# A batch's first two output tiles share their steps, and the first transfers come in another order

## The chip, the cores and the metric

The kernel runs on one core of one Trainium2 chip. The time is the device time of one execution in microseconds (us). Six engines' rows occur here: PE (TensorE's matmuls), PEld (its weight loads), DVE (VectorE), ACT (ScalarE), POOL (GpSimd) and SP (SyncE, which issues most of the transfers; SPq is its queue). Each engine works off its own instructions in the order in which the program lists them, and semaphores hold an instruction back until what it needs is there.

## The reference

```python
# q, k, v: 8 batches, 12 heads, 448 tokens, 64 dims, float32
scores = q @ k.transpose(0, 1, 3, 2) / sqrt(64) - log(448)
x = (sigmoid(scores) @ v)                  # per head
x = x.transpose(0, 2, 1, 3).reshape(3584, 768)
h = x @ w_in                               # 768 x 2048
g = where(h > 0, h, exp(min(h, 0)) - 1)
out = g @ w_out                            # 2048 x 768
```

## The kernel before

**Tiling.** A batch's 448 tokens are three chunks of 128 (`NC` = 3) and a rest of 64; the rests of two batches share one tile. Heads go in pairs, six a batch (`hp` = 0 to 5, `n` counts the pairs over all batches). For a pair, PE multiplies q by k (tile `psc`, L663), ACT takes the sigmoid into `sg` (L687), ACT and DVE turn that into `at` (L698, L699), and PE multiplies `at` by the values (`pav`, L712). After a batch's six pairs its hidden layer follows: PE makes `h` (L1006), and ACT and DVE turn it into `g` in 16 blocks `f` (L1032, L1038); the last quarter, blocks 12 to 15, is put into `left_of_g` and done later, at the start of the next batch's loop.

**The second product.** `moe2(b)` makes the output tiles of batch b, 128 tokens by 384 columns each. An output tile `po` has 16 *steps*, one for each block f, and a step is three matmuls (L1118). After its last step DVE scales it into `o` (L1128) and SP stores it. The `po` tiles are in two PSUM buffers (tag "pm", `PB` = 2), so a third tile can be begun only when DVE has emptied the first. `moe2` is a generator, and its steps are placed in between the attention of the next batch: in the loop for batch b, `fill(n)` issues n steps of batch b-1. The loop's pair 0 issues 5 and then 6 steps; `SHARES` says how many the pairs then have (14, 17, 17, 17, 8 where b-1 is even; 17, 19, 20, 20, 18 where it is odd), and `GAPS` how many of these stand in the pair's first places (0, 7, 0, 1 in even pairs, 0, 4, 0, 1 in odd ones), the others at its end.

**The first stage.** Batches 0 and 1 have no earlier batch beside them; instead w_in (in parts of 1.5 MB) and w_out are loaded and brought into their 16-bit form. Its order on all engines is written out as the string `ORDER`. The tokens that matter here: q0, k0, v0 load a pair's rows (96 KB for each head's half); `n0` and `i0` load the values' and the queries' and keys' rests of batch 0; `l0` loads a part of w_in and `A0` is the first ACT operation on it (L222); `T0` transposes a pair on PE (L1289), `Y0` copies it out of PSUM on ACT (L1305), `S0.0`, `G0.0` and `V0.0` are scores, sigmoid and values of one chunk. All transfers from HBM are issued on SP's queue. Before the first token ACT does one sigmoid on a small constant (`warm`).

Of the kernel before, what the change touches and what calls it, by code (L numbers as in the profile page):

```python
# [11 lines left out]
F32 = mybir.dt.float32  # L12
# [3 lines left out]
AF = mybir.ActivationFunctionType  # L16
# [6 lines left out]

UNITS = 0, 4, 8
ORDER = """
n0 q0 q1 v0 i0 k0 T0 k1 T1 Y0 S0.0 v1 l0 Y1 i1 G0.0 S0.1 q2 q3 V0.0 S1.3 G0.1 S0.2 G1.3
V0.1 l1 v2 S1.0 A0 G0.2 S1.1 V0.2 M0 v3 G1.0 b0 V1.0 Q0 S1.2 B0 G1.1 v13 G1.2 k2 k3 V1.1
N0 V1.2 A1 V1.3 l2 M1 b1 C0 v12 D0 H1 d0 T2 v4 T3 Q1 Y2 v5 S2.0 Y3 G2.0 n1 H0 B1 S2.1 N1
q5 C1 q4 I0 S2.2 G2.1 D1 S3.3 M2 V2.0 E0 G2.2 F0 S3.0 V2.1 I1 G3.3 S3.1 V2.2 G3.0 V3.0
# [36 lines left out]
def attention_ffn(  # L66
# [9 lines left out]
    nc = tc.nc  # L76
    B, H, S, D = q.shape
    DM, DF = w_in.shape
    P = 128
    NP = H // 2  # L80
    NC = S // P
    SM = NC * P
    R = S - SM
    NF = DF // P
# [4 lines left out]
    WF = 2  # L89
    WR, WT = 3, 2  # L90
    WHOLE = 2
# [7 lines left out]
    PB = 2  # L99
# [13 lines left out]
    ps = ctx.enter_context(tc.tile_pool(name="ps", bufs=1, space=PSUM))  # L113

    bias = const.tile([P, 1], F32, name="bias")
# [1 line left out]


    warm = const.tile([P, 1], F32, name="warm")
    nc.scalar.activation(warm, bias, AF.Sigmoid)  # L120
    space = const.tile([P, 2 * NK * DF], F16, name="wi")
    NU = NF // WF
    wi = space.rearrange("p (u h f c x) -> p u h f c x", u=NU, h=2, f=WF, c=NK)
# [28 lines left out]
    ones = const.tile([P, P], BF16, name="ones")  # L152
# [184 lines left out]
    def w_in_ratios():  # L337
        joint_scales(slice(UNITS[1] * WF, UNITS[2] * WF))
        nc.vector.tensor_reduce(wm[:, 0:1], wq, axis=AX.X, op=ALU.max)
        nc.vector.reciprocal(wm[:, 1:2], wm[:, 0:1])  # L340
        nc.gpsimd.tensor_scalar(wn, wq, wm[:, 1:2], 2.0**WTOP, op0=ALU.mult, op1=ALU.mult)
        nc.gpsimd.tensor_tensor(wt, wp, wr, op=ALU.mult)
# [85 lines left out]
    def make_sums(n=1):  # L428
        if not made:
            made.append(sums_of_parts())  # L430
        for _ in range(n):
            store_sums()
            next(made[0], None)
# [69 lines left out]
    def w_out_scale(i):  # L503
        sum_magnitude(wop[:, i : i + 1], out_sums[i][:, :HM])
        s = out_scales[i] = sb.tile([P, 1 + NF], F32, tag="swo", name=f"swo{i}", bufs=2)
        nc.vector.reciprocal(s[:, 0:1], wop[:, i : i + 1])
        nc.vector.tensor_scalar(s[:, 1:], wn, s[:, 0:1], None, op0=ALU.mult)
# [602 lines left out]
    def moe2_tile(wo, rows, lh, sc, i, u, apart):  # L1110


        cols = slice(i * HM, (i + 1) * HM)
        po = ps.tile([P, 512], F32, tag="pm", name=f"po{u}", bufs=PB)
        n = 0
        for f in range(NF):
            for gj, wj in ((0, 0), (0, 1), (1, 0)):
                nc.tensor.matmul(  # L1118
                    po[:, :HM], lh(gj, f), wo[:, i, f, wj],
                    start=(n == 0), stop=(n == 3 * NF - 1),  # L1120
                )
                n += 1
            if f < NF - 1:
                yield

        def store():
            o = sb.tile([P, HM], F32, tag="o", name=f"o{u}", bufs=OB)
            nc.vector.tensor_scalar(o, po[:, :HM], sc, None, op0=ALU.mult)  # L1128
            for pp, dst in rows:
                nc.sync.dma_start(dst[:, cols], o[pp])  # L1130

        if apart is not None:
            apart.append(store)
        else:
            store()
        yield
# [18 lines left out]
    def moe2(b, g, wo, apart=None):  # L1155
        j = b % 2
        osc = oscs[0]

        def tokens(b, c):
            if c < NC:  # L1160
                return out[b * S : b * S + SM].rearrange("(p c) m -> c p m", c=NC)[c]
            return out[b * S + SM : (b + 1) * S]

        def tile_of(c, i):
            if c < NC:
                return moe2_tile(
                    wo, [(slice(0, P), tokens(b, c))],
                    lambda gj, f: g[:, gj, f, c * P : (c + 1) * P],
                    osc[:, j, i : i + 1], i, f"{b}_{c}_{i}", apart,
                )  # L1170
            return moe2_tile(
                wo, [(rows[a], tokens(b - 1 + a, NC)) for a in range(2)],
                lambda gj, f: g[:, gj, f, SM:],
                osc[:, 2, i : i + 1], i, f"{b}_r_{i}", apart,
            )

        for i in range(NH):
            tiles = list(range(NC + j))
            if b == B - 1 and i == NH - 1:
                tiles.insert(0, tiles.pop())  # L1180
            for c in tiles:
                yield from tile_of(c, i)

    wo = g = None
    early = sb.tile([P, 2 * NF * (SM + 2 * R) // 2], F32, tag="g", name="early")
# [1 line left out]
    early_rest = early[:, 4 * S :][:, : 2 * WHOLE * H * D]  # L1187
    early_rest = early_rest.rearrange("p (a b h d) -> p a b h d", a=2, b=WHOLE, h=H)

    def load_rests(b, of_values):  # L1190

        dst = early_rest[:, int(of_values), b]
        for i, r in enumerate(rows):
            src = v if of_values else (q, k)[i]
            nc.sync.dma_start(dst[r], src[b, :, SM:].rearrange("h r d -> r h d"))
    pairs = [(b, hp) for b in range(B) for hp in range(NP)]
    loaded, ready = {}, {}
    xh_of, xs_of, pair_at = {}, {}, {}
# [210 lines left out]
    def first_stage():  # L1409
        nonlocal wo, at  # L1410
        units = [w_in_parts(u) for u in range(NF // WF)]
        pieces = [w_out_parts(k) for k in range(len(PIECES))]
        two = {n: pair_parts(n) for n in range(2 * NP + 2)}
        couples = [couple_parts(c) for c in range(NP)]
        layer, tiles, h, st, stores = None, None, None, {}, []
        for token in ORDER.split():
            name = token.rstrip("0123456789.")
            number = token[len(name) :]
            if name in ("l", "A", "b", "B", "C", "D", "d", "E", "F"):
                units[int(number)][name]()  # L1420
            elif name in ("o", "a", "e", "c", "g", "s", "h", "p"):
                k = int(number)
                if wo is None and (name not in ("o", "e") or PIECES[k][2] == 2):
                    wo = sb.tile([P, NH, NF, 2, HM], F16, tag="wo", name="wo")
                pieces[k][name]()
            elif name in ("i", "n"):
                load_rests(int(number), name == "n")
            elif name == "Wn":
                w_in_ratios()
            elif name == "K":  # L1430
                make_sums()
            elif name == "m":
                i = int(number)
                w_out_scale(i)
                out_scale(0, xs_of[0], st["xp"], slice(i, i + 1))
            elif name in ("M", "Q", "N"):
                couples[int(number)][name]()
            elif name in ("S", "G", "V"):
                n, t = number.split(".")
                two[int(n)][name](int(t))  # L1440
            elif name in ("R", "Rq", "Rr", "x", "y", "j", "z", "w"):
                if layer is None:
                    st, layer = first_layer_parts()
                layer[name](*[int(number)] if number else [])
            elif name == "r":
                if h is None:
                    h = hidden(1)
                next(h)
            elif token == f"P{2 * NP}":
                for n in (2 * NP, 2 * NP + 1):  # L1450
                    loaded[n] = two[n]["state"]["raw"], two[n]["state"]["rv"]
                at = 2 * NP
                measure_next()
            elif name == "X":
                if tiles is None:
                    tiles = moe2(0, g, wo, stores)
                next(tiles)
            elif name == "O":
                stores[int(number)]()
            else:  # L1460
                two[int(number)][name]()
        return h
# [26 lines left out]
    order = {1: [scale_next, make_sums], 3: [split_next, make_sums], 4: [measure_next, make_sums], 6: [scale_next, make_sums], 8: [split_next, make_sums], 10: [make_sums] * 2, 12: [make_sums] * 2, 13: [make_sums] * 2, 14: [measure_next, make_sums], 15: [make_sums] * 2}  # L1489
# [15 lines left out]
    with tc.manual_schedule(engines={E.PE, E.Activation, E.DVE, E.SP, E.Pool}):  # L1505
        h = first_stage()
        of_moe2 = next(h)
        for b in range(2, B):
            out_scale(*of_moe2)
            tiles = moe2(b - 1, g, wo)  # L1510
            left = NF * NH * (NC + (b - 1) % 2)

            def fill(n):
                nonlocal left
                left -= n
                for _ in range(n):
                    next(tiles, None)
# [3 lines left out]
            for hp in range(NP):  # L1521
                n = b * NP + hp
                last = hp == NP - 1
# [16 lines left out]
                if prev:  # L1540
                    for t in range(NC):
                        prev.values(t)
                else:
                    fill(6)
                if hp % 2 == 0:
                    first = p
                    if prev:
# [67 lines left out]
        for _ in moe2(B - 1, g, wo):  # L1615
            pass
# [30 lines left out]
```

## Time and profile before

| what | us |
|---|---|
| median of 3 runs | 1138.45 (1135.16 to 1138.53) |
| the profiled execution | 1137.94 |
| its span, first to last instruction | 1136.1 |
| PE busy in it | 1108.8 (98%) |
| DVE, ACT, POOL busy | 815.6 (72%), 765.3 (67%), 119.4 (11%) |

A row of a timeline gives the start, the length, the engine, the line, the operation and its tiles, and how many instructions it joins; in square brackets stands how long the engine was idle ahead of it and what it waited for. A row of the windows view gives a stretch, its length, then the busy time of PE, PEld, DVE, ACT and POOL with their instructions, the granted clock of TensorE, the mean share of the 16 DMA engines, and GB/s.

### The profile page before, as it was taken

What the parts mean: (1) busy time and instruction counts of PE and PEld (TensorE: products, weight loads), DVE (VectorE), ACT (ScalarE), POOL (GpSimd) and SP (SyncE); (2) the same over time, 40 slices, a digit from 0 to 9 for tenths busy, and PEclk for the clock granted to TensorE, in tenths of its full rate; (3) what the DMA queues carried; (4) which work ended last, traced back from release to release, by engine and by line L of the source; (5) the groups of instructions that cost most, each with busy time, mean ns of one, the idle gap of its engine ahead of it and who ended that gap; (6) DMA issues with size and microseconds to landing.
All of it is one profiled execution on the core that took longest, in us unless ns stands there. A gap on an engine that the chain in (4) does not pass through costs nothing.

```text
span 1136.1 us, 22252 instructions
## 1 busy us (share of the span) xinstructions
PE 1108.8 (98%) x8614; PEld 713.6 (63%) x8614; DVE 815.6 (72%) x1689; ACT 765.3 (67%) x1072; POOL 119.4 (11%) x333
## 2 busy tenths in 40 slices
PE   6899999999999999999999999999999999999998
PEld 2333445555555985589555895569655796559865
DVE  2889899888896768866776567876786567875500
ACT  5898787567775578767866467776766568775600
POOL 0000001332330001100110001100110001110000
PEclk9999999999999999999999999999999999999999
DMA  9882743334673784538442494529553195516100
GB/s 237 244 253 71 244 125 116 131 88 123 167 207 104 213 265 76 123 111 273 136 111 55 130 278 126 112 67 296 153 117 89 50 298 147 112 35 215 41 28 28
DMA packets 224090, 164.65 MB, mean 145 GB/s; under 512 B 170096, under 2 KB 189552, under 8 KB 223984
## 3 DMA queue, kind: packets, MB, share of 16 engines
q1 hardware_dynamic: 220400, 152.22, 48.9%
q0 software_dynamic: 3584, 11.01, 2.7%
q8 instruction: 67, 1.10, 0.4%
q14 instruction: 39, 0.32, 0.1%
HBM read 124.65 MB, written 22.02 MB: 129 GB/s over the span
## 4 chain that ended last, share of the span: by engine, by line
PE 68%; ACT 13%; DVE 10%; DMA 5%; issue 2%; SPq 1%; POOL 0%; DVEq 0%; ACTq 0%; POOLq 0%
PE po L1118 27%; PE X L1006 8%; PE psc L663 7%; PE pav L712 7%; PE ph L905 7%; PE po_r L1118 5%; PE Y L1006 2%; ACT sg L687 2%; PE A L1006 2%; PE B L1006 2%; ACT g L1032 2%; DMA wi<-blend 2%; PE pav L730 1%; DVE g L1038 1%; ACT eb L1017 1%
## 5 line engine op out<-in xcount | busy, mean ns | idle before, releaser
L1118 PE MATMUL po<-wo,g 128*128 128x384 f16 x2304 | 386.4, 326 | 2.3 <-DVE g L1038 2.3
L1118 PEld LDWEIGHTS <-g 128*128 128x128 f16 x2688 | 257.3, 98 | 185.9 <-issue 16.8
L1006 PEld LDWEIGHTS <-wi 128*128 128x128 f16 x3024 | 288.2, 98 | 5.3 <-issue 4.4
L699 DVE SCALAR_TENSOR_TENSOR at<-sg,at 128x896 f16<-128x896 f32 x126 | 132.0, 1086 | 55.3 <-ACT at L698 55.3
L687 ACT ACTIVATE sg<-psc,bias,sc 128x896 f32<-128x896 f32 x108 | 114.7, 1090 | 45.8 <-PE psc L663 39.4
L1006 PE MATMUL X<-wi 128*128 128x224 f16 x1296 | 133.0, 259 | 0.4
L698 ACT ACTIVATE at<-sg 128x896 f16<-128x896 f32 x126 | 113.4, 944 | 0.6
L905 PE MATMUL ph<-xh,wi 128*128 128x448 f16 x576 | 110.8, 352 | 0.0
L663 PE MATMUL psc<-qk 64*128 64x448 f16 (+2 forms) x960 | 108.0, 375 | 0.6 <-ACT sg L687 0.2
L626 ACT ACTIVATE nat<-raw,sc 128x384 f16<-128x384 f32 (+1 forms) x108 | 51.5, 533 | 65.3 <-POOL sc L597 63.1
L905 PEld LDWEIGHTS <-wi 128*128 128x128 f16 x576 | 55.9, 98 | 53.0 <-issue 1.4
L597 POOL TENSOR_SCALAR sc<-sc 128x3 f32<-128x3 f32 x36 | 10.4, 288 | 583.9 <-DVE xs L557 408.9
L712 PE MATMUL pav<-at,vn 128*64 128x448 f16 x648 | 68.2, 355 | 0.0
L1118 PE MATMUL po_r<-wo,g 128*128 128x384 f16 x384 | 64.1, 326 | 0.0
L1021 DVE SCALAR_TENSOR_TENSOR eb<-eb,c 128x896 f32<-128x896 f32 x24 | 26.2, 1091 | 49.6 <-ACT c L1018 49.6
L663 PEld LDWEIGHTS <-qk 64*128 64x128 f16 (+1 forms) x864 | 30.6, 97 | 49.2 <-issue 31.3
L1128 DVE TENSOR_SCALAR o<-po,osc 128x384 f32<-128x384 f32 x48 | 29.3, 611 | 38.9 <-PE po L1118 37.7
L629 DVE SCALAR_TENSOR_TENSOR nat<-raw,sc,nat 128x384 f16<-128x384 f32 (+1 forms) x108 | 50.8, 525 | 7.1 <-ACT nat L626 6.7
L712 PEld LDWEIGHTS <-vn 128*64 128x64 f16 x648 | 33.6, 109 | 32.1 <-issue 13.0
L687 ACT ACTIVATE sg<-psc,bias 128x896 f32<-128x896 f32 x42 | 41.3, 1012 | 6.4 <-PE psc L663 6.3
L1006 PE MATMUL X<-xh,wi 128*128 128x224 f16 x432 | 45.4, 259 | 0.0
L1006 PE MATMUL B<-xh,wi 128*128 128x224 f16 x432 | 45.3, 259 | 0.0
(173 smaller groups left out, 1497.2 us busy)
## 6 DMA issues: line engine op xcount, KB each, us to landing
wi<-blend SPq DMA_DIRECT2D x168, 384.0 KB, 4.6
stage<-in_moe_w_in_dram SPq DMA_DIRECT2D x8, 1536.0 KB, 7.9
wo<-in_moe_w_out_dram SPq DMA_DIRECT2D x13, 768.0 KB, 4.8
raw<-in_q_dram SPq DMA_DIRECT2D x96, 96.0 KB, 3.3
raw<-in_k_dram SPq DMA_DIRECT2D x96, 96.0 KB, 3.0
out_dram<-o SPq DMA_DIRECT2D x48, 192.0 KB, 1.9
blend<-room POOLq DMA_DIRECT2D x38, 192.0 KB, 2.4
rv<-in_v_dram SPq DMA_DIRECT2D x36, 192.0 KB, 2.7
```

Source lines behind the costliest of these rows:

```text
L626: nc.scalar.mul(hi, src, s)
L629: nc.vector.scalar_tensor_tensor(lo, src, s, hi, op0=ALU.mult, op1=ALU.subtract)
L663: nc.tensor.matmul(psc[:, j, :S] if g < NC else psc[rows[x], j, :S], kk[rows[j], o], qq[rows[j], :S], start=(n == 0), stop=(n == n_parts - 1),
L687: nc.scalar.activation(sg, psc[:, :, :S], AF.Sigmoid, bias=bias, scale=scale)
L698: nc.scalar.mul(parts[0], sg, 2.0**ATOP)
L699: nc.vector.scalar_tensor_tensor(parts[1], sg, 2.0**ATOP, parts[0], op0=ALU.mult, op1=ALU.subtract)
L712: nc.tensor.matmul(pav[rows[j], :S], vv[i][:, j * NC + g if g < NC else 2 * NC + j], sg[k][:, j], start=(g == 0 and n == 0), stop=False,)
L905: nc.tensor.matmul(ph[:, :S], wi[:, NU - 1 - f // WF, wj, f % WF, c], hidden_of(b, c)[:, xj], start=(n == 0), stop=(n == 3 * NK - 1),)
L1006: nc.tensor.matmul(to[:, j * HS : (j + 1) * HS], block[:, j, wj, c], rhs(k, c, xj), start=(k in (1, 5) and j == 0 and n == 0), stop=(j == ...
L1021: nc.vector.scalar_tensor_tensor(e, e, -1.0, src, op0=ALU.add, op1=ALU.min)
L1118: nc.tensor.matmul(po[:, :HM], lh(gj, f), wo[:, i, f, wj], start=(n == 0), stop=(n == 3 * NF - 1),)
L1128: nc.vector.tensor_scalar(o, po[:, :HM], sc, None, op0=ALU.mult)
```

## The change

It has three parts.

1. `ORDER` begins `q0 k0 v0 q1 k1 T0 Y0 S0.0 T1 v1 l0 n0 i0 G0.0 Y1 i1` in place of `n0 q0 q1 v0 i0 k0 T0 k1 T1 Y0 S0.0 v1 l0 Y1 i1 G0.0`. The queries' and keys' rests of the first four heads of batch 0 go ahead of all this on ScalarE's queue (two transfers of 64 KB); `i0` loads the other eight heads on SP's.
2. Ten products of a constant `ones` (128x128 by 128x512, bf16) stand on PE ahead of the first transposes. Their result is not used.
3. In `moe2` of batches 2 to 7 the first two tiles of an order (chunks 0 and 1, first half of the columns) share their steps: blocks 0 to 11 of the first, 0 to 11 of the second, 12 to 15 of the first, 12 to 15 of the second. `fill(6)` becomes `fill(7)`.

```diff
 ORDER = """
-n0 q0 q1 v0 i0 k0 T0 k1 T1 Y0 S0.0 v1 l0 Y1 i1 G0.0 S0.1 q2 q3 V0.0 S1.3 G0.1 S0.2 G1.3
+q0 k0 v0 q1 k1 T0 Y0 S0.0 T1 v1 l0 n0 i0 G0.0 Y1 i1 S0.1 q2 q3 V0.0 S1.3 G0.1 S0.2 G1.3
...
-    nc.scalar.activation(warm, bias, AF.Sigmoid)
...
         for i in range(NH):
             tiles = list(range(NC + j))
             if b == B - 1 and i == NH - 1:
                 tiles.insert(0, tiles.pop())
-            for c in tiles:
-                yield from tile_of(c, i)
+            order += [(c, i) for c in tiles]
+        if b >= WHOLE:
+            two = [tile_of(*order.pop(0)) for _ in range(2)]
+            last = 2 * WF
+            for n in (NF - last, last):
+                for t in two:
+                    for _ in range(n):
+                        next(t)
+                        yield
+        for c, i in order:
+            yield from tile_of(c, i)
...
-    def load_rests(b, of_values):
+    def load_rests(b, of_values, heads=slice(0, H), queue=nc.sync):
...
+            queue.dma_start(dst[r], src[b, heads, SM:].rearrange("h r d -> r h d"))
...
+        load_rests(0, False, slice(0, 2 * WF), nc.scalar)
+        nc.scalar.activation(warm, bias, AF.Sigmoid)
+        busy = ps.tile([P, 512], F32, tag="pm", name="busy", bufs=PB)
+        for _ in range(10):
+            nc.tensor.matmul(busy, ones, ones[:, :1].to_broadcast([P, 512]), start=True, stop=True)
         for token in ORDER.split():
...
-                load_rests(int(number), name == "n")
+                first = 2 * WF if token == "i0" else 0
+                load_rests(int(number), name == "n", slice(first, H))
...
                 else:
-                    fill(6)
+                    fill(7)
```

The order of the instructions shows where the pieces lie (the changed file's line numbers differ by a few from those of the kernel before). First SP's queue at the start of the program, before; `early` takes the rests and `raw` a pair's rows:

```order
L1195 DMA early_102<-in_v_dram 64x12x64 x2
L516 DMA raw0_0_107<-in_q_dram 128x3x64 x2
L516 DMA raw0_1_110<-in_q_dram 128x3x64 x2
L539 DMA vn0_0_113<-in_v_dram 128x2x192
L1195 DMA early_102<-in_q_dram 64x12x64
L1195 DMA early_102<-in_k_dram 64x12x64
L516 DMA raw0_0_107<-in_k_dram 128x3x64 x2
L516 DMA raw0_1_110<-in_k_dram 128x3x64 x2
L539 DMA vn0_1_143<-in_v_dram 128x2x192
L277 DMA stage_145<-in_moe_w_in_dram 128x6x256
L1195 DMA early_102<-in_q_dram 64x12x64
```

The same place after:

```order
L515 DMA raw0_0_118<-in_q_dram 128x3x64 x2
L515 DMA raw0_0_118<-in_k_dram 128x3x64 x2
L538 DMA vn0_0_123<-in_v_dram 128x2x192
L515 DMA raw0_1_126<-in_q_dram 128x3x64 x2
L515 DMA raw0_1_126<-in_k_dram 128x3x64 x2
L538 DMA vn0_1_152<-in_v_dram 128x2x192
L276 DMA stage_154<-in_moe_w_in_dram 128x6x256
L1204 DMA early_101<-in_v_dram 64x12x64 x2
L1204 DMA early_101<-in_q_dram 64x8x64
L1204 DMA early_101<-in_k_dram 64x8x64
L1204 DMA early_101<-in_q_dram 64x12x64
```

The values' rests move behind the first part of w_in (`stage`), pair 0's keys move up to its queries, and 64 KB each of the queries' and keys' rests are no longer here.

Next PE in the loop for batch 3, in its second pair. In the names of attention tiles stand the chunk (3 for the rests of two pairs), the batch and the pair: `psc33_0` holds the scores of the rests of batch 3's pairs 0 and 1. `po2_1_0` is the tile of batch 2, chunk 1, first half of the columns, and `pb` is a small product of the next pair's scales. Before:

```order
L663 MATMUL psc33_0_4758<-qk3_1_4342 64x448
...
L1118 MATMUL po2_1_0_4644<-wo_1027,g_1152 128x384
...
L191 LDWEIGHTS ones_84
L191 MATMUL pb_4791<-dg_4686,ones_84 128x12 [waits DVE_49]
L1118 LDWEIGHTS g_1152
...
L1118 MATMUL po2_2_0_4853<-wo_1027,g_1152 128x384
```

After:

```order
L662 MATMUL psc33_0_4771<-qk3_1_4355 64x448
...
L1117 MATMUL po2_0_0_4557<-wo_1040,g_1165 128x384
...
L1117 MATMUL po2_1_0_4642<-wo_1040,g_1165 128x384
...
L190 LDWEIGHTS ones_83
L190 MATMUL pb_4807<-dg_4699,ones_83 128x12 [waits DVE_49]
...
L1117 MATMUL po2_2_0_4866<-wo_1040,g_1165 128x384 [waits DVE_49]
```

Between `psc33_0` and `pb` stand four steps in both. Before, all four are of the second tile. After, two are the last of the first tile and two of the second; after `pb` come the second tile's last two, and then the third tile, whose first matmul waits on a semaphore of DVE.

Last, DVE at the same place, from the last `at` of pair 0 (`at23_0`) to the row behind the `at` of the rests (`at33_0`). `dg` is what the product `pb` reads. Before:

```order
L699 SCALAR_TENSOR_TENSOR at23_0_4623<-sg23_0_4621,at23_0_4623 128x896
L1128 TENSOR_SCALAR o2_0_0_4641<-po2_0_0_4544,osc2_4531 128x384
L629 SCALAR_TENSOR_TENSOR nat3_2_4654<-raw3_2_4032,sc3_2_4579,nat3_2_4654 128x384
...
L185 TENSOR_SCALAR dg_4686<-blocks_88,trm_4684 128x12
L699 SCALAR_TENSOR_TENSOR at03_1_4724<-sg03_1_4713,at03_1_4724 128x896
L699 SCALAR_TENSOR_TENSOR at13_1_4727<-sg13_1_4722,at13_1_4727 128x896
L699 SCALAR_TENSOR_TENSOR at23_1_4773<-sg23_1_4756,at23_1_4773 128x896
L699 SCALAR_TENSOR_TENSOR at33_0_4776<-sg33_0_4771,at33_0_4776 128x896
L195 TENSOR_REDUCE al_4793<-pb_4791 128x3
```

After:

```order
L698 SCALAR_TENSOR_TENSOR at23_0_4639<-sg23_0_4637,at23_0_4639 128x896
L628 SCALAR_TENSOR_TENSOR nat3_2_4667<-raw3_2_4045,sc3_2_4592,nat3_2_4667 128x384
...
L184 TENSOR_SCALAR dg_4699<-blocks_87,trm_4697 128x12
L698 SCALAR_TENSOR_TENSOR at03_1_4737<-sg03_1_4726,at03_1_4737 128x896
L698 SCALAR_TENSOR_TENSOR at13_1_4740<-sg13_1_4735,at13_1_4740 128x896
L698 SCALAR_TENSOR_TENSOR at23_1_4786<-sg23_1_4769,at23_1_4786 128x896
L698 SCALAR_TENSOR_TENSOR at33_0_4789<-sg33_0_4784,at33_0_4789 128x896
L1127 TENSOR_SCALAR o2_0_0_4798<-po2_0_0_4557,osc2_4544 128x384
L194 TENSOR_REDUCE al_4809<-pb_4807 128x3
```

The eviction `o2_0_0` moves from behind the first pair's last `at` to behind the four `at` operations of the second pair (`at03_1` to `at33_0`).

## Rows read from the trace of the kernel before

**Rows 1.** the page: busy time, share of the span, instructions of each engine.

```profile
PE 1108.8 (98%) x8614; PEld 713.6 (63%) x8614; DVE 815.6 (72%) x1689; ACT 765.3 (67%) x1072; POOL 119.4 (11%) x333
```

**Rows 2.** what PE waited for over the span: total us, times, longest.

```profile
PE pt L1289 <- DMA raw<-in_q_dram: 6.5, 1, 6.5
PE po L1118 <- DVE g L1038: 2.3, 5, 0.5
```

**Rows 3.** timeline of the start: start us, us, engine, line, what.

```profile
2.23 2.64 SPq L516 DMA_DIRECT2D raw<-in_q_dram  x4
11.32 1.51 PE L1289 MATMUL pt<-ident,raw 128*128 128x128 f32 x6 [0.40 <-DMA raw<-in_k_dram]
12.24 0.91 ACT L1305 COPY early<-pt 128x896 f32<-128x896 f32 x1 [10.02 <-PE pt L1289]
13.62 2.54 PE L663 MATMUL psc<-early 64*128 64x448 f32 x8
```

**Rows 4.** DMA issues up to 12 us: KB each, median us to landing.

```profile
raw<-in_k_dram SPq DMA_DIRECT2D x4, 96.0 KB, 3.5
```

**Rows 5.** busy time by stretch, then granted clock, DMA share, GB/s.

```profile
2.00:12.00 10.00, 2.02 (x8) 1.39 (x9) 0.55 (x1) 0.21 (x2) 0.09 (x1) 1.00 1.05 198
12.00:22.00 10.00, 8.90 (x42) 3.54 (x41) 1.51 (x5) 7.25 (x8) 0.00 (x0) 1.00 1.05 251
22.00:32.00 10.00, 9.50 (x58) 4.14 (x58) 6.75 (x18) 9.28 (x9) 0.00 (x0) 1.00 1.09 332
32.00:38.00 6.00, 5.13 (x32) 1.88 (x30) 5.01 (x15) 5.63 (x7) 0.00 (x0) 1.00 1.08 283
```

**Rows 6.** what SP's queue waited for, 25 to 27.3 us.

```profile
SPq L516 <- DMA stage<-in_moe_w_in_dram: 1.2, 1, 1.2
```

**Rows 7.** timeline from 26 to 31 us, all engines.

```profile
26.93 1.65 ACT L222 ACTIVATE stage<-stage 128x1536 f32<-128x1536 f32 x1
27.53 1.25 DVE L213 TENSOR_REDUCE mx<-vn 128x1 f32<-128x384 f32 x2 [0.40 <-DMA vn<-in_v_dram]
29.90 0.85 PE L1289 MATMUL pt<-ident,raw 128*128 128x128 f32 x6
```

**Rows 8.** chain of waits from 0 to 60 us: start us, us, what.

```profile
20.77 7.43 DMA vn<-in_v_dram
```

**Rows 9.** PE at the start of batch 3, 425 to 433.6 us.

```profile
427.35 6.19 PE L1118 MATMUL po<-wo,g 128*128 128x384 f16 x37 [0.46 <-DVE g L1038]
```

**Rows 10.** PE in batch 3's second pair, 437 to 447 us.

```profile
437.90 2.12 PE L1118 MATMUL po<-wo,g 128*128 128x384 f16 x12
440.00 6.50 PE L1118 MATMUL po<-wo,g 128*128 128x384 f16 x39
446.43 0.74 PE L663 MATMUL psc<-qk 64*128 64x448 f16 x6
```

**Rows 11.** DVE in the same pair, 433 to 447 us.

```profile
434.46 0.61 DVE L1128 TENSOR_SCALAR o<-po,osc 128x384 f32<-128x384 f32 x1
...
439.83 2.08 DVE L699 SCALAR_TENSOR_TENSOR at<-sg,at 128x896 f16<-128x896 f32 x2
442.98 2.09 DVE L699 SCALAR_TENSOR_TENSOR at<-sg,at 128x896 f16<-128x896 f32 x2 [1.06 <-ACT at L698]
```

**Rows 12.** ACT in the same pair.

```profile
441.01 1.10 ACT L687 ACTIVATE sg<-psc,bias,bl 128x896 f32<-128x896 f32 x1 [1.24 <-DVE at L699]
```

**Rows 13.** PE, then DVE, in batch 4's second pair.

```profile
563.74 2.12 PE L1118 MATMUL po<-wo,g 128*128 128x384 f16 x12
...
563.99 0.23 DVE L185 TENSOR_SCALAR dg<-blocks,trm 128x12 bf16<-128x12 bf16 x1
```

**Rows 14.** busy time and granted clock, two stretches.

```profile
41.00:44.00 3.00, 1.07 (x8) 0.23 (x4) 3.00 (x5) 2.42 (x3) 0.00 (x0) 1.00 0.96 290
1134.00:1136.10 2.10, 0.00 (x0) 0.00 (x0) 0.00 (x0) 0.00 (x0) 0.00 (x0) 0.68 0.20 75
```

**Rows 15.** the page's groups: busy us, mean ns, idle before.

```profile
L905 PE MATMUL ph<-xh,wi 128*128 128x448 f16 x576 | 110.8, 352 | 0.0
```

More of the change, by code (lines that the diff above doesn't have):

```diff
@@ L1175, in tile_of @@
             )
+        order = []
         for i in range(NH):
@@ L1188, in attention_ffn @@
     early_rest = early_rest.rearrange("p (a b h d) -> p a b h d", a=2, b=WHOLE, h=H)
-    def load_rests(b, of_values):
-        dst = early_rest[:, int(of_values), b]
+    def load_rests(b, of_values, heads=slice(0, H), queue=nc.sync):
+        dst = early_rest[:, int(of_values), b, heads]
         for i, r in enumerate(rows):
             src = v if of_values else (q, k)[i]
-            nc.sync.dma_start(dst[r], src[b, :, SM:].rearrange("h r d -> r h d"))
+            queue.dma_start(dst[r], src[b, heads, SM:].rearrange("h r d -> r h d"))
     pairs = [(b, hp) for b in range(B) for hp in range(NP)]
```

## The prediction, made before the changed kernel ran

> **What bounds the kernel now.** First the busy times: TensorE works 1108.8 us of a span of 1136.1, 98%, and no other engine over 72% [rows 1]. So only time in which PE stands still can be won, and any new wait of PE is lost unless a later wait of PE gives it back. Next, PE's waits: the largest is the 6.5 us for the first q rows, then the five waits of 0.46 us, 2.3 in sum, in which the second product waits for DVE's L1038, the last quarter of g [rows 2]. One of the five is the wait at the head of batch 3's long stretch of `po` [rows 9].
>
> Third, the start by timeline. SP issues the first four q transfers from 2.23 us on, 0.66 us each; PE's first transposes are at 11.32, and the first scores at 13.62 [rows 3]. Fourth, the windows: the DMA engines are full from 2 to 38 us, at a share of 1.05 to 1.09 [rows 5]. Within that stretch work begins the moment a transfer lands: SP's wait for the second part of w_in (`l1`) [rows 6] ends as ACT's L222 on it (`A1`) starts at 26.93, and DVE's L213 at 27.53 waited for values [rows 7], whose transfer stands in the chain with 7.43 us [rows 8]. So the start runs at the pace of the bytes.
>
> **The transfers' order.** Issue: ahead of the first q in before stand two transfers of rests. Without them, q and k of pair 0, four transfers at 0.66, are issued from about 2.23 − 2 × 0.66 = 0.9 to 3.6 us; the last one issues at 2.9 and lands 3.5 later [rows 4], at 6.4. From the first transposes to the first scores before took 13.62 − 11.32 = 2.30; with the array at its full clock the six transposes take 0.85 in place of 1.51 [rows 3, 7], so 1.64. First scores at 8.0, 5.6 us sooner. That is no gain of the kernel yet. What ACT and PE do sooner ends in front of the second part of w_in, which lands at 26.9 and the values that land at 27.5, and the bytes ahead of these are the same bytes in another order, over engines that are full. From 22 to 32 us ACT is busy 9.28 of 10 us and PE 9.50 [rows 5], at before's times. So the value I take is 0; the bounds are −5.6 (all of it survives) and +1 (two rests of values, issued after the first part of w_in, come late for their users, whose copy `i0` now follows them too). ACT issues two of the rests' transfers at some 0.66 each [rows 3] ahead of its first work, in a wait of 10.02 us that becomes about 5 [rows 3]: hidden.
>
> The Trainium skill, "DMA: Bandwidth & Descriptors", section "Issuing engines are not separate DMA queues", says that transfers issued from another engine still share the same 16 DMA engines, so that a second issuing engine saves issue time and no bandwidth. The share of 1.05 to 1.09 to 38 us agrees [rows 5]; by it the start gives nothing, by the first scores alone it would give 5.6.
>
> **The ten products.** No such row is in before. A product of 448 columns takes 110.8 / 576 = 0.19 us busy [rows 15], one of 512 then 0.22, ten 2.2, and 4.4 if the array is at the lower of its two levels. They end by 6.4, when the first rows land, if they begin by 2. Cover: PE's wait for the first rows. What they can bring is the clock: transposes 0.66 us shorter, counted above, and the scores behind them; both vanish in the same wait for w_in. Value 0, bounds −1 and +1.
>
> **The shared steps, gain.** Tile 0's blocks 12 to 15 come as steps 25 to 28 and not 13 to 16, so the matmuls that waited for the last quarter of g come 12 steps later than before. A step is three matmuls, 6.50 / 13 = 0.5 us [rows 10], so DVE has 6 us more where 0.46 was missing. All five waits go: −2.3 [rows 2]. In batch 2's loop no such wait stands.
>
> **The shared steps, price.** Tile 0 is now finished at step 28 and not 16, and its buffer is the one that the third tile needs at step 33. Four steps lie between, 2 us, in which DVE must come to the eviction. Where does step 28 fall? In batches 3, 5 and 7 (b − 1 even) pair 0 issues 5 + 7 + 14 = 26 steps. So steps 27 to 30 are the four in the gap of pair 1, behind the scores of the rests, and 31 to 33 the first of the pair's end. DVE's list has the eviction behind the four `at` of the pair, and these depend on ACT's sigmoids of the same scores. In batch 3 before, PE starts the four steps at 437.90, the rest at 440.00 [rows 10]. With two steps to go, PE is at step 33 at 440.00 + 2 × 0.5 = 441.0. DVE works on the first two `at` from 439.83, then waits 1.06 for ACT and works on the second two from 442.98 to 445.07 [rows 11]; ACT's own sigmoid of the rests had to wait 1.24 for DVE to free a buffer [rows 12]. The eviction itself takes 0.61, and its former place at 434.46 falls free, which lets DVE's chain come up to 0.61 sooner [rows 11]. So tile 0's buffer is free at 445.07 + 0.61 − (0 to 0.61), that is 445.1 to 445.7, and PE has stood for 4.1 to 4.7 us. I take 4.2. Behind the waiting matmul stand the other `po` steps of the pair and then the scores at 446.43 [rows 10], which before wait for nothing; PE has no later wait that gives this back. The pattern comes three times (batches 3, 5, 7, the others near 704 and 968 us): 3 × 4.2 = +12.6. Bounds: 0, if the buffer is free in time after all, and 3 × 4.7 = 14.1.
>
> In batches 4 and 6 pair 0 issues 5 + 7 + 17 = 29, the eviction stands in DVE's list right behind pair 1's `dg`, which ends at 563.99 + 0.23 = 564.22 [rows 13]; with 0.61 the buffer is free at 564.8. PE's four steps from 563.74 are now 30 to 33, so 33 comes at 563.74 + 3 × 0.5 = 565.2: 0.4 us to spare. Value 0, up to +1 for each. After the last loop nothing lies beside the steps, and 2 us cover an eviction of 0.61. fill(7) adds a step where fill(6) stood; it moves three matmuls ahead of other ones, and costs nothing by itself.
>
> **The clock.** The row from 41 to 44 us has PE busy 1.07 of 3.00 and a granted clock of 1.00, the last 2.1 us of the span, with no matmul, 0.68 [rows 14]: the array fell to the lower level there. After the first scores no idle stretch of PE before is as long as 4.2 us. If the clock falls in such a stretch, the work behind it runs at half pace for a time. Its price from the start, where the array came from rest: the transposes and the eight scores took 1.51 + 2.54 = 4.05 us [rows 3], at most half of which is loss, 2.0. Bounds 0 and 3 × 2.0 = 6.0; I take two falls of three, +4.0.
>
> The Trainium skill, "TensorE: Matmul & The Clock Gate", section "HAM oscillation — how this bites in real kernels", speaks against this part of the change: idle stretches between bursts of matmuls put the array back to its lower clock each time. By it all three fall and the sum is 2.0 higher, 1154; by the rows from 41 to 44 us alone none falls, and it is 1148 [rows 14].
>
> **Sum**, against the profiled execution's 1137.94 (its span is 1136.1; the median of the runs is 1138.45, half a microsecond off): −2.3 + 0 + 0 + 12.6 + 4.0 = +14.3, so 1152.
>
> **Rivals.**
> A, *the start survives*. ACT and PE carry their 5.6 us past the second part of w_in, since they are nearly full from 22 us on and would have less left to do [rows 5]. For it: 6.75 of 10 us of DVE and 9.28 of ACT there. Against: L222 starts at the landing [rows 6, 7]. 1152.2 − 5.6 = 1146.6.
> B, *the third tile does not wait*: DVE comes to the eviction by 441.0. For it: a list of DVE is not its time, and ACT's and DVE's waits of 1.24 and 1.06 could shrink. Against: four `at` of 1.04 each lie ahead of it from 439.83 on. Start nothing: 1137.94 − 2.3 = 1135.6, no change.
> C, the other side: *no wait and the start survives*. What decides is one thing, that PE's work sets the pace at both places and not what it waits for: 1137.94 − 2.3 − 5.6 = 1130.0, faster. It holds if PE goes past 26.9 us with its lead, and if the eviction is done before 441.0.
> D, *more waits*: the 0.4 us to spare in batches 4 and 6 are gone as well, each with some 2 us and a fall of the clock, in both: 1152.2 + 2 × 2 + 2.0 + 2.0 = 1160.
>
> **How the numbers follow.** What a measurement of this kernel can tell from no change is about 0.3%, 3.4 us: 1135.0 to 1141.9. The forecast has 0.68, A 0.15, B 0.06, C 0.06, D 0.05. The forecast, A and D are slower: 0.88; B is the same, C faster. The forecast's own range is 1146 (no fall of the clock, bounds of start and gap) to 1156; to A's side it goes on to 1143, to D's to 1157. Left out are B, C, most of D: under 2 in 10.
>
> **What would show it.** In the list of PE's waits the row "po <- DVE g L1038" is gone and a row "po <- DVE o", of the eviction's line, stands there with 3 times and some 4 us each, on the third tile, near 441, 709 and 977 us. The granted clock in the 4 us behind each is under 1.00 for at least two. PE's first scores are near 8 us, yet L222 starts on the second part of w_in at 26.9 as before, within 1 us. It is wrong if PE has no wait over 2 us in the loops, or if the work after 45 us runs several microseconds ahead of before.

## The result and the profile after

The changed kernel took 1152.16 us in the median of four runs (1150.50 to 1153.08), the kernel before, run beside it, 1137.96 (1135.16 to 1138.53): 1.0128 of it, 95% interval 1.0106 to 1.0150, slower by 14.2 us. The span of its profiled execution is 1151.3 us. These are PE's largest waits in it, with the total, the times and the longest:

```profile
PE po L1117 <- DVE o L1127: 12.5, 3, 4.2
PE psc L662 <- ACT sg L686: 4.3, 3, 3.1
PE pt L1298 <- DMA raw<-in_k_dram: 3.5, 3, 3.0
PE psc L662 <- ACT early L1314: 2.8, 2, 1.8
```

The five waits for g [rows 2] are gone, and three for an eviction stand in their place. Here is PE at the first of them, in pair 1 of batch 3, where before it went through without a stop [rows 10]:

```profile
436.40 2.12 PE L1117 MATMUL po<-wo,g 128*128 128x384 f16 x12
438.36 0.17 PE L190 MATMUL pb<-dg,ones 128*128 128x12 bf16 x1
438.39 1.14 PE L1117 MATMUL po<-wo,g 128*128 128x384 f16 x6
443.68 6.55 PE L1117 MATMUL po<-wo,g 128*128 128x384 f16 x29 [4.16 <-DVE o L1127]
```

And DVE in the same stretch [rows 11]:

```profile
437.86 2.09 DVE L698 SCALAR_TENSOR_TENSOR at<-sg,at 128x896 f16<-128x896 f32 x2
441.01 2.10 DVE L698 SCALAR_TENSOR_TENSOR at<-sg,at 128x896 f16<-128x896 f32 x2 [1.06 <-ACT at L697]
443.02 0.61 DVE L1127 TENSOR_SCALAR o<-po,osc 128x384 f32<-128x384 f32 x1
```

The two rows are to be read against each other: the first tile's last step is issued in the group of twelve from 436.40, so its sums are ready before 439 us, but DVE, which works its list off in order, comes to the eviction only at 443.02. PE starts 0.05 us after its end. The other two waits are the same to 0.01 us (they end at 712.26 and 981.92).

The clock behind the first wait and behind the second, by windows (length, busy PE, PEld, DVE, ACT, POOL, granted clock, DMA share, GB/s):

```profile
438.00:443.60 5.60, 1.53 (x11) 0.81 (x9) 4.54 (x6) 3.10 (x4) 0.00 (x0) 1.00 0.50 114
443.60:446.00 2.40, 2.32 (x11) 1.25 (x11) 1.51 (x9) 1.33 (x4) 1.30 (x5) 0.76 0.33 112
446.00:448.00 2.00, 2.00 (x8) 0.92 (x7) 2.00 (x5) 0.70 (x2) 0.22 (x1) 0.50 0.00 0
448.00:450.00 2.00, 2.00 (x13) 1.21 (x12) 1.85 (x7) 0.00 (x0) 0.00 (x0) 0.94 1.09 207
...
712.00:714.00 2.00, 1.74 (x6) 0.84 (x6) 1.11 (x8) 0.75 (x2) 0.81 (x4) 0.50 0.29 100
714.00:716.00 2.00, 2.00 (x8) 0.88 (x6) 2.00 (x5) 1.27 (x3) 0.71 (x3) 0.50 0.03 6
716.00:718.00 2.00, 2.00 (x8) 0.94 (x7) 1.93 (x5) 0.00 (x0) 0.00 (x0) 0.52 0.77 148
```

In 446 to 448 us PE is busy throughout and issues 8 matmuls: the array is at 0.50 of full speed, the lower of its two levels. A busy share of 100% hides this; the count and the clock show it. Behind the second wait the lower level lasts longer, through all three windows, and behind the third it is the same (0.50 from 981.9 to 986 us, 0.61 in the two after).

At the start the first scores come at 7.32 us in place of 13.62 [rows 3], and ACT begins on the second part of w_in at 27.39 in place of 26.93 [rows 7]. The first two rows are PE's, the others ACT's:

```profile
7.32 1.02 PE L662 MATMUL psc<-early 64*128 64x448 f32 x4 [0.99 <-ACT early L1314]
...
30.77 0.85 PE L1298 MATMUL pt<-ident,raw 128*128 128x128 f32 x6 [2.96 <-DMA raw<-in_k_dram]
...
15.63 1.58 ACT L221 ACTIVATE stage<-stage 128x1536 f32<-128x1536 f32 x1 [2.26 <-DMA stage<-in_moe_w_in_dram]
...
27.39 1.59 ACT L221 ACTIVATE stage<-stage 128x1536 f32<-128x1536 f32 x1 [2.75 <-DMA stage<-in_moe_w_in_dram]
```

The lead of 6.3 us is spent in waits for transfers that before had no wait ahead of them; at PE's `pb` near 45 us (45.42 in place of 46.13) 0.7 of it is left.

### The profile page after: what moved, and what is told of

Read it like the earlier page. It is cut to its first block, busy times and chain, and to the rows that moved or that the text cites. A ratio compares the mean times of both kernels' runs of the same rounds, so it can differ in the third digit from the quotient of the medians.

```text
span 1151.3 us, 22276 instructions
## 1 busy us (share of the span) xinstructions
PE 1119.9 (97%) x8624; PEld 716.9 (62%) x8624; DVE 816.4 (71%) x1689; ACT 765.1 (66%) x1072; POOL 118.9 (10%) x333
## 4 chain that ended last, share of the span: by engine, by line
PE 79%; DVE 6%; ACT 5%; DMA 5%; SPq 2%; issue 1%; DVEq 0%; ACTq 0%
PE po L1117 26%; PE X L1005 13%; PE ph L904 9%; PE psc L662 7%; PE pav L711 7%; PE po_r L1117 5%; PE Y L1005 3%; PE A L1005 3%; PE B L1005 3%; DMA wi<-blend 2%; DVE at L698 2%; ACT sg L686 1%; PE pav L729 1%; DMA raw<-in_k_dram 1%; SPq L515 1%
## 5 line engine op out<-in xcount | busy, mean ns | idle before, releaser
L1117 PE MATMUL po<-wo,g 128*128 128x384 f16 x2304 | 392.3, 331 | 12.5 <-DVE o L1127 12.5
L662 PEld LDWEIGHTS <-qk 64*128 64x128 f16 (+1 forms) x864 | 30.5, 97 | 49.6 <-issue 33.0
L1005 PE MATMUL Y<-xh,wi 128*128 128x224 f16 x432 | 45.3, 260 | 0.0
```

What stands on the lines that cost most here:

```text
L662: nc.tensor.matmul(psc[:, j, :S] if g < NC else psc[rows[x], j, :S], kk[rows[j], o], qq[rows[j], :S], start=(n == 0), stop=(n == n_parts - 1),
L1005: nc.tensor.matmul(to[:, j * HS : (j + 1) * HS], block[:, j, wj, c], rhs(k, c, xj), start=(k in (1, 5) and j == 0 and n == 0), stop=(j == ...
L1117: nc.tensor.matmul(po[:, :HM], lh(gj, f), wo[:, i, f, wj], start=(n == 0), stop=(n == 3 * NF - 1),)
```

## The experiments

All were timed in five rounds beside the kernel before; the medians of before were 1138.20 (first four), 1138.09 (next four) and 1138.03 (last two).

**The start alone.** `if False:` in place of `if b >= WHOLE:` in `moe2`, and `fill(6)`:

```diff
-        if b >= WHOLE:
+        if False:
...
-                    fill(7)
+                    fill(6)
```

> Parts 1 and 2 of the change (transfers' order, two transfers on ScalarE's queue, ten products) on the kernel before; the output tiles one after the other as before. Theory (the start runs at the pace of the bytes, and the lead of the first scores is lost in front of the second part of w_in): first scores near 7.3 us, ACT's L221 on the second part of w_in near 27.4 as in the changed kernel, time within 1.5 us of before, about -1.0. Rival A (the start survives): -5.6 us. Rival (the changed kernel's loss is in the start: PE's two idle stretches of 3 us there, with the clock down behind each): +3 us or more.

Measured: 1136.75 us, 0.9988 (0.9978 to 0.9998), or 1.4 us faster; first scores at 7.88, ACT on the second part of w_in at 27.39 after a wait of 3.09. Rival A, 5.6 us, is out: the first scores are 5.7 sooner and the end 1.4, so some 4 us of the lead are lost, and what is left is at the edge of what can be told from nothing. The start is not where the changed kernel loses either. The trace puts still less of the gain at the start. PE's `pb` near 46 us stands here in the kernel before, in this kernel and in the third one below, which has the start of before:

```profile
46.13 0.18 PE L191 MATMUL pb<-dg,ones 128*128 128x12 bf16 x1
...
45.60 0.18 PE L190 MATMUL pb<-dg,ones 128*128 128x12 bf16 x1
...
45.45 0.18 PE L191 MATMUL pb<-dg,ones 128*128 128x12 bf16 x1
```

With the old start one execution is as early there as with the new one.

**The shared steps alone.** The changed kernel with before's `ORDER` line, its `warm` sigmoid back in its old place, `i0` whole, and without these lines:

```diff
-        load_rests(0, False, slice(0, 2 * WF), nc.scalar)
...
-        for _ in range(10):
-            nc.tensor.matmul(busy, ones, ones[:, :1].to_broadcast([P, 512]), start=True, stop=True)
```

> Part 3 alone (shared steps, fill(7)) on the kernel before's start. Theory (three waits of the third tile for the eviction, 4.15 us each, and a fall of the clock behind each that costs 2 us more; five waits for g gone, -2.3): +15 to +17 us against before, three waits 'po <- DVE o' of 4.1 us in the trace. Rival (the clock comes back at once, only the gaps cost): +10 us. Rival (the shared steps are harmless alone): within 2 us of before.

Measured: 1153.14 us, 1.0127 (1.0104 to 1.0149). PE's waits:

```profile
PE po L1118 <- DVE o L1128: 12.5, 3, 4.2
```

So this part alone makes the whole loss; 15 us are more than the three gaps.

**Two steps moved.** The eviction gets ahead of the four `at` if the first tile ends in pair 0. The same edit on the shared steps alone and on the whole change:

```diff
-    SHARES = (14, 17, 17, 17, 8), (17, 19, 20, 20, 18)
+    SHARES = (16, 15, 17, 17, 8), (17, 19, 20, 20, 18)
```

> Part 3 alone, with two steps more in pair 0 and two fewer in pair 1 of the loops for batches 3, 5 and 7 (SHARES 16, 15, 17, 17, 8 in place of 14, 17, 17, 17, 8), so that step 28, the first tile's last, ends pair 0 and its eviction stands ahead of pair 1's four 'at' in DVE's list. Theory: no wait of the third tile over 0.5 us, the waits for g gone: -2 to -3 us against before, 17 to 19 us under part 3 alone. Rival (the sharing itself costs, by its weight loads or its two open tiles): over +5 us.

Measured: 1133.38 us, 0.9961 (0.9948 to 0.9974), 4.8 us faster than before, near twice what was expected. PE is ahead of before already at a `pb` in the hidden layer of batch 2, where no step is shared yet:

```profile
398.89 0.17 PE L191 MATMUL pb<-dg,ones 128*128 128x12 bf16 x1
...
397.55 0.17 PE L191 MATMUL pb<-dg,ones 128*128 128x12 bf16 x1
```

These 1.3 us are not the sharing's. What the two moved steps do without shared steps was not run.

> The whole change, with the same two steps moved from pair 1 to pair 0. Theory (the sum of the start alone and the moved sharing): -3 to -4 us against before, 1134 to 1135 us. Rival A (the start survives once the waits are away): -8 us.

Measured: 1132.93 us, 0.9954 (0.9938 to 0.9971), 5.3 us faster than before and 19 under the change as it was. This is the best kernel of the study, by 0.4 us, which the runs cannot tell from nothing, ahead of the shared steps alone with the same move. PE and then DVE in pair 1 of batch 3 of the whole change with the steps moved:

```profile
437.87 2.12 PE L1117 MATMUL po<-wo,g 128*128 128x384 f16 x12
439.83 0.17 PE L190 MATMUL pb<-dg,ones 128*128 128x12 bf16 x1
439.86 5.52 PE L1117 MATMUL po<-wo,g 128*128 128x384 f16 x33
...
438.33 0.23 DVE L184 TENSOR_SCALAR dg<-blocks,trm 128x12 bf16<-128x12 bf16 x1
438.47 0.61 DVE L1127 TENSOR_SCALAR o<-po,osc 128x384 f32<-128x384 f32 x1
439.00 2.08 DVE L698 SCALAR_TENSOR_TENSOR at<-sg,at 128x896 f16<-128x896 f32 x2
```

The eviction is done at 439.08, ahead of the work on the `at`, and PE goes on without a wait.

**One step moved.** Does each step by which the first tile ends sooner buy its half microsecond, or is it the place in DVE's list?

```diff
-    SHARES = (14, 17, 17, 17, 8), (17, 19, 20, 20, 18)
+    SHARES = (15, 16, 17, 17, 8), (17, 19, 20, 20, 18)
```

> The whole change with one step moved from pair 1 to pair 0 and not two (SHARES 15, 16, 17, 17, 8): step 28 is now the second of pair 1's four, and the eviction still stands behind the four 'at' in DVE's list. Theory (the place in DVE's list decides, not the number of steps between): the three waits stay, 4.1 to 4.7 us each, 1152 to 1154 us. Rival (each step of distance buys its half microsecond, and two moved steps just sufficed): the waits are half as long, some 1142 us.

Measured: 1153.01 us, 1.0130 (1.0116 to 1.0144). The waits are not halved:

```profile
PE po L1117 <- DVE o L1127: 12.8, 3, 4.3
```

It is the place in DVE's list. With one step moved, step 28 is the first of pair 1's four (the expectation calls it the second), and the eviction still comes behind the four `at`, from 443.34 to 443.95; PE goes on at 444.00 and has waited as long. With two steps moved the eviction comes ahead of the four `at`, and the wait is gone. In all three kernels four steps lie between step 28 and step 33.

**The idle time filled.** In the whole change, 36 products without use behind `pb`, in other columns of its PSUM bank, in batches 3, 5 and 7:

```diff
             nc.tensor.matmul(pb[:, : n * 4], ones, dg.rearrange("p n x -> p (n x)"), start=True, stop=True)
+            for _ in range(extra.pop() if extra else 0):
+                nc.tensor.matmul(
+                    pb[:, 256:512], ones, ones[:, :1].to_broadcast([P, 256]), start=True, stop=True,
+                )
...
+                        if hp == 1 and b % 2:
+                            extra.append(36)
```

> The whole change, with 36 products of the constant (256 columns each, some 0.107 us each at the full clock, 3.84 us in sum, results unused) put on PE behind pb in pair 1 of batches 3, 5 and 7, where PE stood still. The third tile is released by DVE as before, so the order and the wait's end are the same; only the idle time is filled. Theory (each standstill costs 4.3 us in itself and some 2.0 us more by the fall of the clock behind it): the wait for the eviction shrinks to under 1 us, the granted clock stays at 1.00 behind it, and the time is 5 to 6.5 us under the changed kernel's, 1146 to 1147 us. Rival (the extra 2 us come from something else behind the standstill, such as DVE's or ACT's later work): the time stays at 1152 us.

Measured: 1146.40 us, 1.0070 (1.0058 to 1.0083), 5.8 us under the changed kernel. PE at the first place, and the clock behind it:

```profile
438.74 0.17 PE L190 MATMUL pb<-dg,ones 128*128 128x12 bf16 x1
438.77 4.16 PE L192 MATMUL pb<-ones 128*128 128x256 bf16 x36
442.77 1.14 PE L1121 MATMUL po<-wo,g 128*128 128x384 f16 x6
444.06 4.22 PE L1121 MATMUL po<-wo,g 128*128 128x384 f16 x25 [0.16 <-DVE o L1131]
```

```profile
444.00:446.00 2.00, 1.94 (x12) 1.17 (x12) 1.11 (x8) 0.95 (x3) 0.94 (x5) 1.00 0.28 100
446.00:448.00 2.00, 2.00 (x15) 1.21 (x13) 2.00 (x5) 1.08 (x2) 0.59 (x2) 1.00 0.00 0
```

The third tile starts when it did, 5.32 us behind `pb` in both kernels (438.74 to 444.06 here, 438.36 to 443.68 there), and yet the kernel is faster by 5.8 / 3 = 1.9 us for each place. That this is the clock can be read from one `pb` to the next, a stretch with the same work but for the useless products. Here it is at the second place, before, in the changed kernel and in the filled one:

```profile
703.97 0.17 PE L191 MATMUL pb<-dg,ones 128*128 128x12 bf16 x1
718.28 0.17 PE L191 MATMUL pb<-dg,ones 128*128 128x12 bf16 x1
...
706.94 0.17 PE L190 MATMUL pb<-dg,ones 128*128 128x12 bf16 x1
728.33 0.17 PE L190 MATMUL pb<-dg,ones 128*128 128x12 bf16 x1
...
705.73 0.17 PE L190 MATMUL pb<-dg,ones 128*128 128x12 bf16 x1
724.36 0.17 PE L190 MATMUL pb<-dg,ones 128*128 128x12 bf16 x1
```

The stretch lasts 14.31, 21.39 and 18.63 us. The filled kernel loses 4.32, the wait alone; the changed one loses 2.76 more. At the first place these 2.76 are 1.68, at the third 2.75: 7.2 in sum, where the medians say 5.8. The windows of the changed kernel say the same: at a clock of 0.50 half of the time is lost, which is 1.74 × 0.50 + 2.00 × 0.50 + 2.00 × 0.48 = 2.8 at the second place and 2.40 × 0.24 + 2.00 × 0.50 + 2.00 × 0.06 = 1.7 at the first. So the useless products buy back what the clock costs, and the 4.3 us of each place stay.

**The start's parts**, on the whole change with the steps moved (1132.93). Without the ten products:

```diff
-        for _ in range(10):
-            nc.tensor.matmul(busy, ones, ones[:, :1].to_broadcast([P, 512]), start=True, stop=True)
```

> The whole change with the two steps moved (as the kernel that took 1132.93), without the ten products. Theory (the start's lead is lost in front of the second part of w_in, so the products bring nothing that lasts): within 1 us of the kernel with them, 1132 to 1134 us; first scores up to 2 us later. Rival (a warm array at the start is worth its 1.2 us to the end): 1134 to 1135 us.

Measured: 1133.37 us. First scores at 7.86 (8.07 with the products), four of them in 1.86 us in place of 1.02: the products do make them faster, and nothing of it shows at the end.

With 14 and 12 more products in the start's two standstills (a token U issues so many):

```diff
-V0.1 l1 v2 S1.0 A0 ... D0 H1 d0 T2 ...
+V0.1 l1 v2 S1.0 U14 A0 ... D0 H1 d0 U12 T2 ...
```

> The same kernel with 14 and 12 more products of 512 columns on PE in the start's two standstills (behind the first scores of pair 1, and ahead of pair 2's transposes), where the trace of the change shows granted clocks of 0.54 at 18 to 20 us and 0.50 at 33 to 35 us. Theory: the first changes nothing (the second part of w_in lands no sooner), the second saves what the array loses from 30.8 to 35 us, at most 2 us, if PE and not the transfers sets the pace from 31 to 44 us: 1131 to 1133 us. Rival (PE isn't the bound until 48 us): no change, 1133 us.

Measured: 1134.51 us. The granted clock is now 1.00 in every window from 15 to 37 us. In the changed kernel's trace it was 0.54 at 18 to 20 and 0.50 at 33 to 35; in the trace of the kernel that this one is built on only the second standstill shows a fall, 0.56 from 30.5 to 33 and 0.70 from 33 to 35. The last stretch, there and here:

```profile
33.00:35.00 2.00, 2.00 (x8) 0.85 (x8) 2.00 (x3) 1.23 (x2) 0.00 (x0) 0.70 1.06 388
...
33.00:35.00 2.00, 1.28 (x10) 0.59 (x9) 1.93 (x4) 1.77 (x3) 0.00 (x0) 1.00 1.07 376
```

A full clock there gains nothing that shows; PE now stands for a third of this stretch.

The rests of batch 0 whole on SP's queue, behind pair 0's keys:

```diff
-        load_rests(0, False, slice(0, 2 * WF), nc.scalar)
...
-q0 k0 v0 q1 k1 T0 Y0 S0.0 T1 v1 l0 n0 i0 G0.0 ...
+q0 k0 i0 v0 q1 k1 T0 Y0 S0.0 T1 v1 l0 n0 G0.0 ...
```

> The same kernel as the one that took 1132.93, with the two rests' transfers of 64 KB gone from ScalarE's queue and batch 0's queries' and keys' rests whole on SP's queue behind pair 0's keys. Theory (the first scores' lead doesn't last): first scores 1.5 to 3 us later, time within 1 us, 1132 to 1134 us. Rival (the second queue is what gives the start's 1.4 us): 1134 to 1135 us.

Measured: 1134.06 us, with the first scores at 10.81 and not 8.07: 2.7 us of lead less, 1.1 us of time, and that inside the spread of the runs.

The second part of w_in ahead of the rests of batch 1:

```diff
-... G0.0 Y1 i1 S0.1 q2 q3 V0.0 S1.3 G0.1 S0.2 G1.3 V0.1 l1 v2 ...
+... G0.0 Y1 l1 i1 S0.1 q2 q3 V0.0 S1.3 G0.1 S0.2 G1.3 V0.1 v2 ...
```

> The whole change with the two steps moved (1132.93), and in the transfers' order the second part of w_in (token l1) ahead of batch 1's queries' and keys' rests and of pairs 2 and 3's queries. Theory (the start runs at the pace of all its bytes): the wait of 4.33 us for this part goes, ACT starts on it at about 23 us, but the keys and values of pairs 2 and 3 land later by what was moved ahead, and the time stays within 1 us, 1132 to 1134 us. Rival A in another form (the start's lead of 5 us is lost in this one wait alone): 1129 to 1130 us.

Measured: 1134.94 us. ACT starts on this part at 25.56 without a wait in front (27.26 after 4.33 in the kernel that it is built on). PE's transposes of pairs 2 and 3, in the kernel that it is built on and then in this one:

```profile
30.66 1.42 PE L1298 MATMUL pt<-ident,raw 128*128 128x128 f32 x6 [4.57 <-DMA raw<-in_k_dram]
...
31.68 0.85 PE L1298 MATMUL pt<-ident,raw 128*128 128x128 f32 x6 [2.85 <-DMA raw<-in_k_dram]
33.24 0.87 PE L1298 MATMUL pt<-ident,raw 128*128 128x128 f32 x3 [0.60 <-DMA raw<-in_k_dram]
```

The expectation of 23 us was too early, since ACT waited for PE's scores first. With the wait for this part gone, PE still stands in front of the keys of pairs 2 and 3, as in the kernel that it is built on, and the time is not better. That the keys come 1.0 us later here is not shown to be the edit's: SP's queue is 0.9 us behind (16.11 in place of 15.24) already where the two orders part.

## Why the prediction came out

- *The wait for the buffer*: taken at 4.2 us, three times, on the third tile; measured as idle 4.15 to 4.16, three times, there. From the start of one matmul to the start of the next it is 4.48 us against 0.16 within a group, so 4.32 of loss each, 13.0 in sum. The working holds in its parts too: DVE begins its first `at` 1.46 us behind PE's four steps (436.40 to 437.86) and before 1.93 (437.90 to 439.83), 0.47 sooner where 0 to 0.61 was allowed, and its wait for ACT stays 1.06. Rival B (DVE comes in time) is out. Rival D too: batches 4 and 6 show no such wait.
- *The clock*: two falls of three at 2.0 us were taken, +4.0; it fell three times, at 1.7, 2.8 and 2.8 us in the profiled execution and 5.8 in sum by the medians with the waits filled. The price was near, the number was a guess between three and none, and it was one short. The Trainium skill, "TensorE: Matmul & The Clock Gate", section "HAM oscillation — how this bites in real kernels", has the array fall back at each idle stretch between bursts, so all three by it; behind each of the three waits of 4.15 us a window shows 0.50, so the trace agrees.
- *The waits for g*: gone, as forecast, but −2.3 was too small. In the kernel before, the matmul behind each of the five waits starts 0.785 to 0.786 us after the one ahead of it, in place of 0.162: 0.62 lost each, 3.1 in sum, where the idle time in [rows 2] said 0.46. The shared steps with two steps moved gained 4.8 (3.0 to 5.9 by the interval). In its profiled execution 1.3 of that stands ahead of the first shared step; of the other 3.5 these waits explain 3.1, and 0.4 stays open.
- *The start*: 0 was taken, −1.4 measured for the start alone, between the bounds −5.6 and +1. The mechanism (the lead is lost in front of transfers) is in the trace, and the kernel with the part of w_in early shows that it isn't that one transfer: with its wait gone, PE stands in front of the next keys all the same. What the small gain consists of, the runs can't tell, nor whether it is the start's: near 46 us the trace shows 0.5 us of it, and an execution with the old start is as far ahead there.
- *The sum*: in the two profiled executions PE's last `pb` stands at 1045.39 and before at 1030.09, 15.3 us sooner. Ahead of the shared steps the changed kernel is 1.4 sooner (397.46 in place of 398.89), the three places take 13.0 + 7.2, and the rest is −3.5, of which the waits for g are 3.1. Against the forecast's +14.3 that is +0.4 for the waits, +3.2 for the clock, −1.2 for g and the rest, −1.4 ahead of the shared steps: +1 in all, and the median of the runs lies 0.9 below the profiled execution. So the wait, its place and its number were forecast; that 1152 was met so closely is partly luck, since a third fall of the clock and two longer ones were made up by terms that were taken too small or at nothing.

## What to carry to other kernels

When a tile is finished later, look for who needs its buffer next, and for the place of its eviction in the other engine's list; the distance in the producer's own steps says little: it was four steps in all three kernels here, and one step moved changed nothing while two gained 19 us. Price an idle stretch of TensorE with what follows it: 4.3 us of standing cost 6.0 to 7.1. A lead at a start that is paced by transfers shows early in the trace and ends at the next transfer.

## What was not expected of the hardware

The idle time that the trace shows ahead of a matmul is less than what is lost. A matmul's row lasts 326 ns, the next one starts 162 ns after it began, and an idle of 0.46 us is counted from the row's end; from start to start the loss was 0.62.

Three waits of the same length (4.15 us) had different prices: behind the first the array lost 1.7 us by its clock, behind the others 2.8.

Products whose result nobody reads, written to other columns of a PSUM bank in use, kept the granted clock at 1.00 over a wait of 4 us, and were worth 5.8 us in a kernel of 1152. The expectation of that run had 5 to 6.5 for it.
